# Moving lower-part subtractions between VectorE and GpSimd in the first 24 steps of a two-layer kernel

## The chip, the core and the metric

The kernel runs on one core of one Trainium2 chip. The metric is the device time of one execution in microseconds (us), given as the median of three runs. The engines are named as in the profile: PE is the matrix engine (TensorE) and PEld its weight loads, DVE is VectorE, ACT is ScalarE, POOL is GpSimd, and SP is SyncE, which only issues DMAs here. DMAs move data between the chip's memory and the on-chip memory SBUF. PE writes to PSUM, which has eight banks here: four for the first product of a step ("ps") and four for the second ("acc").

## The reference

The inputs are eight batches of eight heads with 576 positions of width 64, and two feed-forward layers with weights of 512 x 2048 and 2048 x 512 in float64 (they reach the kernel as pairs of 32-bit words).

```
q_s = exp(q - max(q, width));      q_s = q_s / sum(q_s, width)
k_s = exp(k - max(k, positions));  k_s = k_s / sum(k_s, positions)
x   = q_s @ (k_s^T @ v)                      # per head; 4608 tokens x 512
h   = x @ w_in;   g = where(h > 0, h, exp(min(h, 0)) - 1);   x = g @ w_out      # layer 1 (elu)
h   = x @ w2_in;  g = (a0 + a1 h + a2 h^2 + a3 h^3) / (1 + |b0||h| + |b1| h^2 + 1e-6)
out = g @ w2_out                                                                # layer 2 (rational)
```

## The kernel before, in words

**Blocks and steps.** The 4608 tokens are cut into nine blocks of 512 (index j), the 2048 hidden values into 16 slices of 128 (index f). A step is one layer, one block and one slice. Its "in" part makes h of 128 hidden values by 512 tokens in one ps bank (12 matmuls, L781 to L783), and its "out" part adds the slice's share to four acc banks (12 matmuls, L823). There are 144 steps in each layer. The list `tiles` sets their order; steps are numbered from 0 in that order, and I5 and O5 below are the in and out parts of step 5. Steps 0 to 3 are block 0 with slices 0 to 3, steps 4 to 11 are block 1 with slices 0 to 7, steps 12 to 23 finish block 0, and steps 24 to 31 finish block 1.

**Two parts of each number.** A float32 matrix is split into an upper part of fewer bits and a lower part, the difference. Each product is three matmuls: upper by upper, upper by lower, lower by upper. ACT makes the upper part (`copy_hi`, L299), and `sub_lo` (L302) subtracts it on the engine that it is given. So L302 stands for the lower part of an elu tile ("gs<-m,gs"), of an input tile ("xs<-ps,xs") or of weights ("w_in<-x,w_in" and "w_out<-x,w_out").

**An elu step.** When h is there, ACT makes relu(-h) in a tile m (L887) and its exponential (L890), DVE makes the elu from m and h and so frees the ps bank (L893), ACT makes the upper part in a tile gs (L299), and then comes the lower part from m and gs (L302), which frees m. Out matmuls read gs and free it. There are two m tiles, two gs tiles and four ps banks: the relu of a step waits for the lower part of the step two earlier, and an in part waits for the elu four earlier.

**Weights of layer 1.** They are loaded as 64-bit words in pairs of slices: one tile of 1 MB for w_in and one for w_out, so 16 tiles in all. A conversion is five operations: a guard of the high half words on DVE ("floor", L323), a scaling on ACT (L331), a shift on DVE (L327), a join on DVE (L335), the upper part on ACT (L299, 128 x 1024), and then the lower part (L302, 128 x 1024). Pair 0 is wanted at I0, pair 1 at I2, pairs 2 and 3 at I8 and I10, and the others at I16, I18, I20 and I22; the w_out tiles are wanted at the out parts of the same steps.

**Attention.** It is made beside the steps. For each pair of heads k goes through a maximum (L667), an exponential (L670), transposes (L679) and the product with v (L518); q goes through a maximum (L537), a subtraction (L560, POOL), an exponential (L564), a sum (L567), its reciprocal (L571, L572), a multiplication (L575, POOL) and transposes (L581). L637 then makes a block's x of two pairs of heads at a time, and ACT and DVE (L302, "xs<-ps,xs") split it.

**What sets the order.** The instructions are not written out in order. `op` registers an operation with the engines it may use, an estimated cost, what it waits for, the buffers that it takes and frees, and a rank. `Plan.run` then lists them: at each turn it starts the operation that can begin first by its own clock, and settles ties by due times that `set_due` works out backward from the order of the PE work. `EITHER` lets the planner choose POOL (1.4) or DVE (0.8). Each engine executes its list in order, so a waiting instruction holds up all behind it on that engine. L276 are matmuls of an identity that the planner puts in where it sees PE wait in the first 100 us.

Of the kernel before, what the change touches and what calls it, by code (L numbers as in the profile page):

```python
# [34 lines left out]
class Plan:  # L35
# [17 lines left out]
    def op(self, engines, fn, after=(), rank=0.0, take=(), free=(), extra=0.0, follow=(), dma=0.0):  # L53
        o = dict(lead=self.lead, rush=0.0, main=False, due=None, follow=[a for a in follow if a is not None], issued=None, engines=engines, fn=fn, after=[a for a in after if a is not None], rank=rank, take=take,
                 free=free, extra=extra, dma=dma, held={}, end=None, next=[], n=len(self.ops))
        waits = o["after"] + o["follow"]
        o["left"] = len(waits)
        for a in waits:
            a["next"].append(o)
        self.ops.append(o)  # L60
        return o
# [120 lines left out]
def linear_attention_elu_rational(  # L182
# [65 lines left out]
    op = plan.op  # L248
# [7 lines left out]
    def DVE(c=0.75):  # L256
        return (("DVE", c),)

    def ACT(c=0.62):
        return (("ACT", c),)  # L260

    def POOL(c=1.4):
        return (("POOL", c),)

    EITHER = (("POOL", 1.4), ("DVE", 0.8))
# [5 lines left out]
    def f32_tile(tag, bufs, pool=None):  # L271
        return (pool or main).tile([P, TB], F32, tag=tag, name=tag, bufs=bufs)
# [25 lines left out]
    def copy_hi(hi, src):  # L298
        nc.scalar.activation(out=hi, in_=src, func=AF.Copy)  # L299

    def sub_lo(e, lo, src, hi):
        engine[e].tensor_tensor(out=lo, in0=src, in1=hi.bitcast(F32), op=ALU.subtract)  # L302
# [4 lines left out]
    def new_slots(f, which):  # L307
        pair = main.tile([P, 2, 2, DM], F32R, tag=f"w{f // 2}_{which}", name=("w_in", "w_out")[which], bufs=1)
        for i in range(2):
            slot[f + i, which] = pair[:, i]  # L310
        return pair

    def whole(n):
        return 0.2 + n * 0.0006, 0.2 + n * 0.00116

    def plan_f32(st_op, st_of, new_x, n, rank, x_kinds, joined=None):

        b = {}
        fast, slow = whole(n)

        def floor(e):
            top = st_of().rearrange("p n t -> p (n t)").bitcast(I16).rearrange("p (n u) -> p n u", u=4)[:, :, 3]
            nc.vector.tensor_scalar(out=top, in0=top, scalar1=FLOOR, scalar2=None, op0=ALU.max)  # L323

        def low(e):
            t = st_of()[:, :, 0]
            nc.vector.tensor_scalar(out=t, in0=t, scalar1=29, scalar2=None, op0=ALU.logical_shift_right)  # L327

        def scale(e):
            b["x"] = new_x()  # L330
            nc.scalar.activation(out=b["x"], in_=st_of()[:, :, 1].bitcast(F32), func=AF.Prelu, scale=2.0**-112, alpha=-2.0**32)  # L331

        def join(e):
            xi = b["x"].bitcast(I32)
            nc.vector.scalar_tensor_tensor(out=joined().bitcast(I32) if joined else xi, in0=xi, scalar=3, in1=st_of()[:, :, 0], op0=ALU.logical_shift_left,  # L335
                                           op1=ALU.bitwise_or)

        o1 = op(DVE(slow), floor, [st_op], rank)
        o2 = b["own"] = op(ACT(0.25 + n * 0.00095), scale, [o1], rank, take=x_kinds)
        o3 = op(DVE(fast), low, [st_op], rank)  # L340
        return op(DVE(slow), join, [o2, o3], rank), b

    def plan_w1(f, which, rank, load_rank, after):

        w = (moe_w_in, moe_w_out)[which]
        kind = f"w{f // 2}_{which}"
        b = {}

        def load(e):
            b["st"] = main.tile([P, 2 * DM, 2], I32, tag=kind, name="bits", bufs=1)  # L350
            nc.sync.dma_start(out=b["st"].rearrange("p n t -> p (n t)"), in_=w[f // 2].bitcast(I32))

        def new_x():
            (name, _), = x["own"]["held"].items()
            return at.tile([P, 2 * DM], F32, tag=name, name="x", bufs=1)

        def pairs(ap):
            return ap.rearrange("p (i n) -> p i n", i=2)

        def hi(e):  # L360
            b["hl"] = new_slots(f, which)
            copy_hi(b["hl"][:, :, 0], pairs(x["x"]))

        def lo(e):
            sub_lo(e, b["hl"][:, :, 1], pairs(x["x"]), b["hl"][:, :, 0])

        b["op"] = op(SP, load, after, load_rank, take=[kind], dma=2.6)
        o, x = plan_f32(b["op"], lambda: b["st"], new_x, 2 * DM, rank, [("x", "st")])
        own = op(ACT(1.05), hi, [o], rank)
        o = op(DVE(1.4), lo, [own], rank, free=[(("x", "st"), x["own"])])  # L370
        at_ops.append(o)
        for i in range(2):
            slot_ready[0, f + i, which], slot_owner[0, f + i, which] = o, b["op"]
        return o
# [391 lines left out]
    def step_of(L, j, f):  # L766
        return place[L, j, f]

    def plan_in(t, b):
        L, j, f = t  # L770
        s = step_of(*t)

        def mm(kks):
            def fn(e):
                if 0 in kks:
                    b["h"] = bank()
                w = slot[f, 0].rearrange("p s (k c) -> p s k c", c=P)
                for kk in kks:
                    x = x_tile[L, j, kk]
                    o = turned(b["h"])  # L780
                    nc.tensor.matmul(o, w[:, 0, kk, :], two(x[:, 0]), start=(kk == 0), stop=False)  # L781
                    nc.tensor.matmul(o, w[:, 0, kk, :], two(x[:, 1]), start=False, stop=False)  # L782
                    nc.tensor.matmul(o, w[:, 1, kk, :], two(x[:, 0]), start=False, stop=(kk == KD - 1))  # L783
            return fn

        parts = [(i,) for i in range(KD)] if f in (0, KF - 1) else [tuple(range(KD))]
        o = None
        for n, kks in enumerate(parts):
            free = []
            if f == KF - 1:  # L790
                free += [(x_owner[L, j, kk][0], x_owner[L, j, kk][1]) for kk in kks]
            if j == NB - 1 and n == len(parts) - 1 and f % 2:
                free.append((f"w{f // 2}_0", slot_owner[L, f, 0]))
            o = op(PE(0.65 * len(kks)), mm(kks),
                   [last.get("mm_in"), slot_ready[L, f, 0]] + [x_ready[L, j, kk] for kk in kks],
                   s, take=["bank"] if n == 0 else [], free=free,
                   follow=[x_owner[L, j, kk][1] for kk in range(KD)] if n == 0 and f == 0 else [])
            o["main"] = True
            if n == 0:
                b["h_op"] = o  # L800
            last["mm_in"] = o
        in_ops[t] = o
        return o
# [77 lines left out]
    def plan_elu(t):  # L881
        b = {}
        s = step_of(*t)

        def relu(e):
            b["m"] = f32_tile("m", 2)
            nc.scalar.activation(out=b["m"], in_=b["h"], func=AF.Relu, scale=-1.0)  # L887

        def exp(e):
            nc.scalar.activation(out=b["m"], in_=b["m"], func=AF.Exp, scale=-1.0)  # L890

        def elu(e):
            nc.vector.scalar_tensor_tensor(out=b["m"], in0=b["m"], scalar=-1.0, in1=b["h"], op0=ALU.add, op1=ALU.max)  # L893

        def hi(e):
            b["g"] = main.tile([P, 2, TB], F32R, tag="gs", name="gs", bufs=2)
            copy_hi(b["g"][:, 0], b["m"])

        def lo(e):
            sub_lo(e, b["g"][:, 1], b["m"], b["g"][:, 0])  # L900

        o = plan_in(t, b)
        o1 = op(ACT(), relu, [o], s + 0.5, take=["m"])
        o = op(ACT(), exp, [o1], s + 0.6)
        o = op(DVE(), elu, [o], s + 0.7, free=[("bank", b["h_op"])])
        o2 = op(ACT(), hi, [o], s + 1.0, take=["gs"])
        b["g_op"] = op(EITHER, lo, [o2], s + 1.1, free=[("m", o1)])
        b["g_free"] = ("gs", o2)
        plan_out(t, b)

# [90 lines left out]
    for n in range(2 * KF):  # L1001
        f, which = divmod(n, 2)
        s = KF + 3 * n
# [9 lines left out]
    for f in range(KF):  # L1013
        for which in range(2):
            b = {}
# [6 lines left out]
            own = slot_owner.get((1, f - 1, which))  # L1022
# [12 lines left out]
            own = op(ACT(), hi, [l, own if f % 2 else None], r, take=[] if f % 2 else [kind])  # L1035
# [33 lines left out]
    with tc.manual_schedule():  # L1069
# [25 lines left out]
        o = op(SP, load_ab, [in_ops[0, 1, 0]], 0.0)  # L1095
        op(ACT(0.2), minus_a, [o, in_ops[0, 2, 0]], 0.0)
        o = op(ACT(0.2), abs_b1, [o, in_ops[0, 2, 0]], 0.0)
        o = op(DVE(0.1), seed_b1, [o], 0.0)
        for _ in range(3):
            o = op(DVE(0.5), heron, [o], 0.0)  # L1100
# [69 lines left out]
```

## Time and profile before

| what | us |
|---|---|
| three runs | 1595.84, 5881.48, 1594.9 |
| median | 1595.84 |
| profiled execution, its own time | 1596.48 |
| its span, first to last instruction | 1594.7 |
| PE busy | 1572.8 (99% of the span) |
| DVE busy | 1039.8 (65%) |
| ACT busy | 1041.5 (65%) |
| POOL busy | 763.6 (48%) |

PE is busy nearly throughout, and the others half to two thirds of the span. These shares are means over stages: in the first 130 us DVE is nearly as full as PE. An idle time in square brackets at a row's end is that of the engine before the instruction, with what ended it. Durations of matmuls overlap, since they are pipelined; one starts about every 0.216 us when nothing holds PE up.

### The profile page before, as it was taken

How to read it: one execution, taken by the hardware profiler on the slowest of the kernel's cores; microseconds unless marked ns; L12 is line 12 of the kernel's file. 1: busy time of each engine (PE TensorE's matmuls, PEld its weight loads, DVE VectorE, ACT ScalarE, POOL GpSimd, SP SyncE). 2: the span in 40 equal slices, each digit the busy share in tenths (PEclk: the TensorE clock that was granted, in tenths of full speed). 3: DMA queues.
4: the chain of work that ended last, by engine and by line, in shares of the span. 5: the costliest groups of instructions: out<-in, count | busy, mean ns of one | idle time of the engine just before them, and what ended most of it. 6: DMA issues, size and time to landing. Idle time of an engine off the chain costs nothing.

```text
span 1594.7 us, 22842 instructions
## 1 busy us (share of the span) xinstructions
PE 1572.8 (99%) x8370; PEld 1355.0 (85%) x8370; DVE 1039.8 (65%) x1624; ACT 1041.5 (65%) x1837; POOL 763.6 (48%) x552
## 2 busy tenths in 40 slices
PE   8999999999999999999999999999999999999998
PEld 7787888888888888888887888888888888888886
DVE  7887666564655556431227768687778687777776
ACT  6767655454655455444558767777777777777676
POOL 3333323232332222232657566656666656666554
PEclk9999999999999999999999999999999999999999
DMA  9513443232332322101422010101010000100000
GB/s 348 221 67 102 144 142 110 90 110 97 102 111 88 102 96 90 53 14 34 139 93 80 1 54 1 54 0 54 0 54 1 28 27 20 34 7 21 1 27 27
DMA packets 48784, 113.31 MB, mean 71 GB/s; under 512 B 5664, under 2 KB 5664, under 8 KB 46624
## 3 DMA queue, kind: packets, MB, share of 16 engines
q1 hardware_dynamic: 48672, 111.85, 20.3%
q8 instruction: 66, 1.08, 0.3%
q14 instruction: 46, 0.38, 0.1%
HBM read 82.47 MB, written 29.36 MB: 70 GB/s over the span
## 4 chain that ended last, share of the span: by engine, by line
PE 87%; issue 3%; ACT 3%; DVE 3%; POOL 2%; DMA 0%; POOLq 0%; SPq 0%; DVEq 0%; ACTq 0%
PE acc L823 43%; PE ps L781 14%; PE ps L782 14%; PE ps L783 14%; POOL gs L302 2%; PE ps L637 1%; PE ps L510 1%; ACT p L926 1%; ACT s L922 1%; ACT m L932 0%; DMA e<-in_q_dram 0%; ACT m L935 0%; DVE s L938 0%; DVE m L941 0%; ACT g L299 0%
## 5 line engine op out<-in xcount | busy, mean ns | idle before, releaser
L781 PE MATMUL ps<-xs,w_in 128*128 128x512 f32 x1152 | 439.6, 382 | 6.6 <-DVE m L893 3.6
L782 PE MATMUL ps<-xs,w_in 128*128 128x512 f32 x1152 | 438.5, 381 | 0.0
L783 PE MATMUL ps<-xs,w_in 128*128 128x512 f32 x1152 | 438.4, 381 | 0.0
L823 PE MATMUL acc<-gs,w_out 128*128 128x512 f32 x1728 | 403.9, 381 | 1.3 <-POOL gs L302 0.8
L823 PEld LDWEIGHTS acc<-gs,w_out 128*128 128x128 f32 x1728 | 324.0, 189 | 52.9 <-ACT gs L299 2.8
L302 POOL TENSOR_TENSOR gs<-m,gs 128x512 fp32r<-128x512 f32 x119 | 163.4, 1373 | 360.5 <-ACT gs L299 336.6
L781 PEld LDWEIGHTS ps<-xs,w_in 128*128 128x128 f32 x1152 | 218.7, 190 | 42.0 <-issue 6.5
L783 PEld LDWEIGHTS ps<-xs,w_in 128*128 128x128 f32 x1152 | 218.7, 190 | 31.3
L782 PEld LDWEIGHTS ps<-xs,w_in 128*128 128x128 f32 x1152 | 218.7, 190 | 31.3 <-DVE xs L302 0.3
L893 DVE SCALAR_TENSOR_TENSOR m<-m,ps 128x512 f32<-128x512 f32 x144 | 98.4, 684 | 207.2 <-ACT m L890 198.5
L302 POOL TENSOR_TENSOR gs<-p,gs 128x512 fp32r<-128x512 f32 x72 | 115.9, 1609 | 236.1 <-issue 197.5
L929 POOL TENSOR_TENSOR s<-s,m 128x512 f32<-128x512 f32 x144 | 218.5, 1517 | 16.9 <-ACT m L918 16.9
L823 PE MATMUL acc<-w_out,gs 128*128 128x512 f32 x864 | 202.4, 381 | 2.7 <-ACT gs L299 1.6
L823 PE MATMUL acc<-w_out,g 128*128 128x512 f32 x864 | 199.8, 379 | 0.5 <-POOL g L302 0.5
L887 ACT ACTIVATE m<-ps 128x512 f32<-128x512 f32 x144 | 85.8, 596 | 167.2 <-PE ps L783 126.9
L938 DVE SCALAR_TENSOR_TENSOR s<-s,m 128x512 f32<-128x512 f32 x144 | 142.6, 990 | 71.6 <-ACT m L935 71.6
L823 PEld LDWEIGHTS acc<-w_out,gs 128*128 128x128 f32 x864 | 162.9, 189 | 29.4 <-POOL gs L302 4.6
L823 PEld LDWEIGHTS acc<-w_out,g 128*128 128x128 f32 x864 | 163.2, 189 | 24.0 <-POOL g L302 0.9
L926 ACT ACTIVATE p<-ps,a_sb 128x512 f32<-128x512 f32 x144 | 112.2, 779 | 81.4 <-POOL gs L302 74.0
L299 ACT ACTIVATE gs<-m 128x512 fp32r<-128x512 f32 x144 | 90.4, 628 | 92.4 <-PE acc L823 78.5
L947 DVE SCALAR_TENSOR_TENSOR p<-p,a_sb,ps 128x512 f32<-128x512 f32 x144 | 107.4, 746 | 57.1 <-ACT m L918 57.0
L951 DVE SCALAR_TENSOR_TENSOR p<-p,a_sb,m 128x512 f32<-128x512 f32 x144 | 136.6, 949 | 2.1
(122 smaller groups left out, 1904.7 us busy)
## 6 DMA issues: line engine op xcount, KB each, us to landing
x<-e SPq DMA_DIRECT2D x36, 256.0 KB, 2.1
e<-x SPq DMA_DIRECT2D x36, 256.0 KB, 3.0
out_dram<-e SPq DMA_DIRECT2D x36, 256.0 KB, 2.0
bits<-in_moe_w_in_dram SPq DMA_DIRECT2D x8, 1024.0 KB, 10.4
bits<-in_moe_w_out_dram SPq DMA_DIRECT2D x8, 1024.0 KB, 12.3
st<-in_moe_w_in_dram SPq DMA_DIRECT2D x16, 512.0 KB, 4.4
w<-st SPq DMA_DIRECT2D x32, 256.0 KB, 2.0
st<-in_moe_w_out_dram SPq DMA_DIRECT2D x16, 512.0 KB, 4.7
```

Source lines behind the costliest of these rows:

```text
L299: nc.scalar.activation(out=hi, in_=src, func=AF.Copy)
L302: engine[e].tensor_tensor(out=lo, in0=src, in1=hi.bitcast(F32), op=ALU.subtract)
L781: nc.tensor.matmul(o, w[:, 0, kk, :], two(x[:, 0]), start=(kk == 0), stop=False)
L782: nc.tensor.matmul(o, w[:, 0, kk, :], two(x[:, 1]), start=False, stop=False)
L783: nc.tensor.matmul(o, w[:, 1, kk, :], two(x[:, 0]), start=False, stop=(kk == KD - 1))
L823: nc.tensor.matmul(turned(o), lhsT, two(rhs), start=(f == f0 and n == 0), stop=(f == f1 and n == 2))
L893: nc.vector.scalar_tensor_tensor(out=b["m"], in0=b["m"], scalar=-1.0, in1=b["h"], op0=ALU.add, op1=ALU.max)
L926: nc.scalar.activation(out=b["p"], in_=b["h"], func=AF.Identity, scale=a_sb[:, 3:4], bias=a_sb[:, 2:3])
L929: engine[e].tensor_tensor(out=b["s"], in0=b["s"], in1=b["a"], op=ALU.add)
L938: nc.vector.scalar_tensor_tensor(out=b["s"], in0=b["s"], scalar=1.0 + 1e-6, in1=b["a"], op0=ALU.add, op1=ALU.mult)
L947: nc.vector.scalar_tensor_tensor(out=b["p"], in0=b["p"], scalar=a_sb[:, 1:2], in1=b["h"], op0=ALU.add, op1=ALU.mult)
L951: nc.vector.scalar_tensor_tensor(out=b["p"], in0=b["p"], scalar=a_sb[:, 0:1], in1=b["a"], op0=ALU.add, op1=ALU.mult)
```

## The change

The planner's estimate for a guard, a shift or a join over n values on DVE falls by 0.1 us each (`whole`). The lower parts of all 16 weight tiles of layer 1 go from DVE (estimate 1.4) to POOL (estimate 2.5). The lower parts of elu tiles of steps 0 to 23, for which the planner could choose, are set to DVE (estimate 0.7); before the change it had put all 24 on POOL. Numbers that are computed stay the same.

```diff
     def whole(n):
-        return 0.2 + n * 0.0006, 0.2 + n * 0.00116
+        return 0.1 + n * 0.0006, 0.1 + n * 0.00116
...
         own = op(ACT(1.05), hi, [o], rank)
-        o = op(DVE(1.4), lo, [own], rank, free=[(("x", "st"), x["own"])])
+        o = op(POOL(2.5), lo, [own], rank, free=[(("x", "st"), x["own"])])
...
         o2 = op(ACT(), hi, [o], s + 1.0, take=["gs"])
-        b["g_op"] = op(EITHER, lo, [o2], s + 1.1, free=[("m", o1)])
+        b["g_op"] = op(DVE(0.7) if s < 24 else EITHER, lo, [o2], s + 1.1, free=[("m", o1)])
```

The planner makes other lists from this. On PE the parts I4 to I18 and O4 to O13 stand in the same order in both; after O13 the change puts I19 one part earlier. From about step 95 of 288 on, the lists of all engines are the same again, and so is the whole of layer 2.

POOL before, from the subtraction for the third q tile of block 1 on (L560 and L575 are the attention's, "gs" are elu tiles):

```order
L560 TENSOR_TENSOR qt<-qt,mx 128x512
L302 TENSOR_TENSOR gs<-m,gs 128x512
L575 TENSOR_TENSOR qt<-qt,mx 128x512
L560 TENSOR_TENSOR qt<-qt,mx 128x512
L302 TENSOR_TENSOR gs<-m,gs 128x512
```

and POOL in the change, from the first weight tile on:

```order
L302 TENSOR_TENSOR w_in<-x,w_in 128x2x512
L575 TENSOR_TENSOR qt<-qt,mx 128x512
L302 TENSOR_TENSOR w_out<-x,w_out 128x2x512
L560 TENSOR_TENSOR qt<-qt,mx 128x512
L302 TENSOR_TENSOR w_in<-x,w_in 128x2x512
L575 TENSOR_TENSOR qt<-qt,mx 128x512
L560 TENSOR_TENSOR qt<-qt,mx 128x512 x2
L575 TENSOR_TENSOR qt<-qt,mx 128x512
L302 TENSOR_TENSOR w_out<-x,w_out 128x2x512
```

Where an elu tile of 512 columns stood between two attention operations, a weight tile of 1024 columns stands now; behind this stretch POOL's list has one more L575 and then the other twelve weight tiles, ahead of the attention of block 2.

DVE before, from the elu (L893) of step 12 to that of step 14:

```order
L893 SCALAR_TENSOR_TENSOR m<-m,ps 128x512
L335 SCALAR_TENSOR_TENSOR x<-x,bits 128x1024 x2
L323 TENSOR_SCALAR bits<-bits 128x1024
L893 SCALAR_TENSOR_TENSOR m<-m,ps 128x512
L302 TENSOR_TENSOR w_in<-x,w_in 128x2x512
L302 TENSOR_TENSOR w_out<-x,w_out 128x2x512
L327 TENSOR_SCALAR bits<-bits 128x1024
L323 TENSOR_SCALAR bits<-bits 128x1024
L893 SCALAR_TENSOR_TENSOR m<-m,ps 128x512
```

and DVE in the change, between the same three elus:

```order
L893 SCALAR_TENSOR_TENSOR m<-m,ps 128x512
L335 SCALAR_TENSOR_TENSOR x<-x,bits 128x1024
L302 TENSOR_TENSOR gs<-m,gs 128x512
L327 TENSOR_SCALAR bits<-bits 128x1024
L335 SCALAR_TENSOR_TENSOR x<-x,bits 128x1024
L893 SCALAR_TENSOR_TENSOR m<-m,ps 128x512
L323 TENSOR_SCALAR bits<-bits 128x1024
L302 TENSOR_TENSOR gs<-m,gs 128x512
L327 TENSOR_SCALAR bits<-bits 128x1024
L893 SCALAR_TENSOR_TENSOR m<-m,ps 128x512
```

Two weight tiles have left the place between the elus of steps 13 and 14, and an elu tile's lower part stands in each of the two gaps.

## Rows read from the trace of the kernel before

**Rows 1.** Waits of PE: who waited for whom, us in total, times, longest.

```profile
PE ps L781 <- DVE m L893: 3.6, 2, 2.2
PE ps L781 <- DVE p L947: 3.0, 2, 2.8
```

**Rows 2.** Busy time by stretch: length, then each engine's us (instructions), clock, DMA.

```profile
20.00:65.80 45.80, 42.74 (x351) 34.37 (x349) 44.16 (x68) 34.71 (x58) 19.43 (x13) 1.00 0.66 252
118.80:131.30 12.50, 8.90 (x31) 6.62 (x30) 10.73 (x11) 9.67 (x12) 1.81 (x2) 0.86 0.33 110
```

**Rows 3.** Timeline of PE: start, duration, what; I4, I17 and I18 begin here.

```profile
65.83 0.48 PE L781 MATMUL ps<-xs,w_in 128*128 128x512 f32 x1
...
121.21 0.48 PE L781 MATMUL ps<-xs,w_in 128*128 128x512 f32 x1 [1.38 <-DVE m L893]
...
126.93 0.49 PE L781 MATMUL ps<-xs,w_in 128*128 128x512 f32 x1 [2.21 <-DVE m L893]
```

**Rows 4.** Timeline of DVE, early: first weight guard, lower parts of block 1's input.

```profile
13.60 0.69 DVE L537 TENSOR_REDUCE mx<-e 128x8 f32<-128x512 f32 x1 [1.24 <-DMA e<-in_q_dram]
...
17.10 1.28 DVE L323 TENSOR_SCALAR bits<-bits 128x1024 int16<-128x1024 int16 x1
...
62.63 1.32 DVE L302 TENSOR_TENSOR xs<-ps,xs 128x512 fp32r<-128x512 f32 x2
```

**Rows 5.** DVE groups by line in 16 to 62.6 us: busy us, mean ns, idle.

```profile
L302 DVE TENSOR_TENSOR w_out<-x,w_out 128x1024 fp32r<-128x1024 f32 x2 | 3.1, 1530 | 0.0
...
L302 DVE TENSOR_TENSOR w_in<-x,w_in 128x1024 fp32r<-128x1024 f32 x2 | 2.5, 1234 | 0.0
```

**Rows 6.** Busy time from step 4's elu to step 13's, columns as in Rows 2.

```profile
70.90:120.40 49.50, 48.16 (x221) 41.23 (x219) 41.58 (x36) 32.56 (x41) 18.28 (x8) 1.00 0.31 128
```

**Rows 7.** DVE groups by line in that stretch, columns as in Rows 5.

```profile
L335 DVE SCALAR_TENSOR_TENSOR x<-x,bits 128x1024 int32<-128x1024 int32 x8 | 13.3, 1672 | 1.1 <-ACT x L331 0.7
L323 DVE TENSOR_SCALAR bits<-bits 128x1024 int16<-128x1024 int16 x7 | 10.7, 1522 | 0.0
L327 DVE TENSOR_SCALAR bits<-bits 128x1024 int32<-128x1024 int32 x6 | 6.7, 1134 | 0.0
...
L302 DVE TENSOR_TENSOR w_in<-x,w_in 128x1024 fp32r<-128x1024 f32 x3 | 4.7, 1576 | 0.2 <-ACT w_in L299 0.2
L302 DVE TENSOR_TENSOR w_out<-x,w_out 128x1024 fp32r<-128x1024 f32 x3 | 3.7, 1225 | 0.2 <-ACT w_out L299 0.2
```

**Rows 8.** POOL group by line in that stretch, columns as in Rows 5.

```profile
L302 POOL TENSOR_TENSOR gs<-m,gs 128x512 fp32r<-128x512 f32 x8 | 18.3, 2285 | 39.1 <-ACT gs L299 39.1
```

**Rows 9.** Timeline of DVE: a guard, a pair of joins, the queue before step 14's elu.

```profile
104.96 2.42 DVE L323 TENSOR_SCALAR bits<-bits 128x1024 int16<-128x1024 int16 x1
...
113.84 3.02 DVE L335 SCALAR_TENSOR_TENSOR x<-x,bits 128x1024 int32<-128x1024 int32 x2
116.72 1.37 DVE L323 TENSOR_SCALAR bits<-bits 128x1024 int16<-128x1024 int16 x1
120.47 0.69 DVE L893 SCALAR_TENSOR_TENSOR m<-m,ps 128x512 f32<-128x512 f32 x1 [2.37 <-ACT m L890]
121.07 1.22 DVE L302 TENSOR_TENSOR w_in<-x,w_in 128x1024 fp32r<-128x1024 f32 x1
122.21 2.31 DVE L302 TENSOR_TENSOR w_out<-x,w_out 128x1024 fp32r<-128x1024 f32 x1
...
126.16 0.71 DVE L893 SCALAR_TENSOR_TENSOR m<-m,ps 128x512 f32<-128x512 f32 x1
```

**Rows 10.** Timeline of POOL: two lower parts of elu tiles, steps 9 and 11.

```profile
103.90 2.29 POOL L302 TENSOR_TENSOR gs<-m,gs 128x512 fp32r<-128x512 f32 x1 [5.82 <-ACT gs L299]
...
114.04 5.03 POOL L302 TENSOR_TENSOR gs<-m,gs 128x512 fp32r<-128x512 f32 x1 [3.53 <-ACT gs L299]
```

**Rows 11.** Tile gs up to 180 us: duration ns min, median, max; first, last start.

```profile
L302 POOL TENSOR_TENSOR gs<-m,gs x24: 1276/1380/5032, 36.5 to 174.7; 128x512 fp32r<-128x512 f32 x24
```

**Rows 12.** Timeline of DVE: a lower part of an elu tile on DVE, later.

```profile
206.77 0.68 DVE L302 TENSOR_TENSOR gs<-m,gs 128x512 fp32r<-128x512 f32 x1
```

## The prediction

> **What bounds the kernel now.** I read the page's shares first: PE is busy for 1572.8 us of a span of 1594.7, so the end moves only where PE starts its work earlier or loses less. Next came PE's waits [rows 1]. The reader is to see two entries: 3.6 us for two in parts that waited for an elu (L893, layer 1), and 3.0 us for two that waited for layer 2's DVE work (L947). The second lies where the lists are unchanged, so I let it stand. The first belongs to the change, and PE's timeline places it [rows 3]: I17 waited 1.38 us and I18 2.21 us. The table by stretch shows what this cost (the later stretch of [rows 2]): in 12.5 us PE did 31 matmuls at a granted clock of 0.86. Undisturbed, 221 matmuls took 48.16 us [rows 6], 0.218 us each, so 31 are worth 6.8 us, and 5.7 us were lost. The waits make 3.6 of that. A mean clock of 0.86 over 12.5 us is 3.5 us at the lower level (1.2 of 2.4 GHz), which costs about 1.8 more.
>
> The other loss is at the start. From 20 to 65.8 us DVE was busy for 44.16 of 45.8 us (the earlier stretch of [rows 2]), and PE, though it shows 42.74, filled much of it with identity matmuls and small attention products. I4, the first step on block 1, began at 65.83 [rows 3], just behind the lower parts of block 1's input on DVE, whose first pair stood at 62.63 [rows 4]. From I4 to I17 PE had work without a break worth naming: 48.16 of 49.5 us [rows 6]. So two things count: when I4 starts, and what is lost at I17 and I18.
>
> **Term 1, up to I4.** I count what stands on DVE ahead of block 1's first input pair. Before: six guards, five shifts, five joins, four weight lower parts. After: five, five, four, none, and four elu lower parts. Removed are a guard (1.52) and a join (1.67, [rows 7]), and weight parts of 3.1 + 2.5 = 5.6 us [rows 5]; added are four elu parts at 0.68 [rows 12], 2.7 us. That is -6.1 us. The first guard (1.28) also moves ahead of the maximum at 13.60, into DVE's idle time of 1.24 us before it [rows 4], if its weights have landed by then; another -1.3: -7.4 us if DVE's amount alone decides.
>
> Against it: four weight parts now run on POOL. POOL shows no tile of 1024 columns. An undisturbed elu part takes it 1.28 us [rows 11]; twice that, 2.56, is the upper bound. On DVE the step from 512 to 1024 columns is 0.68 to 1.22 us [rows 9, 12], a factor of 1.79, which gives 2.30 as the lower one. I take 2.43, the middle. POOL then holds what the two engines share for 4 x 2.43 = 9.7 us in place of 4 x 1.28 = 5.1, up to 4.6 us of DVE's time, and the first two weight tiles come 1.2 us later each behind their join. That leaves -7.4 + 4.6 + 2.4 = -0.4, say 0, as the other end. I take the middle, **-3.7 us**.
>
> **Term 2, from step 4's elu to step 13's.** Between those two elus the change's list has two joins and two shifts more than the old one, eight elu lower parts, and no weight lower part (six before). That is 2 x 1.67 + 2 x 1.13 + 8 x 0.68 - (4.7 + 3.7) = +2.6 us [rows 7, 12]. Now the shared port. That the two engines exclude each other can be read: the guard at 104.96 took 2.42 us, against 1.28 for the first one, because POOL's elu part ran until 106.19 [rows 4, 9, 10]; and POOL's part for step 11 took 5.03 us, since DVE ran two joins and a guard beside it [rows 9, 10]. In this stretch POOL held the port for 8 x 1.28 = 10.2 us; nine weight tiles need 9 x 2.43 = 21.9, which is 11.7 us more. What can cover it: nine elus of 0.69 us [rows 9], 6.2 us, which read one tile from PSUM and one from SBUF. DVE's idle 49.5 - 41.58 = 7.9 us [rows 6] covers the rest if DVE fills it. DVE then needs 41.58 + 2.6 + 5.5 to 11.7 = 49.7 to 55.9 us where it took 49.5: +0.2 to +6.4. Nothing says how often POOL meets an elu, so I take the middle, **+3.3 us**. A gain is not in the bounds because DVE has as much of its own to do and POOL more.
>
> A rule of the Trainium skill speaks against the change here (SBUF — State Buffer, section "Who interferes with whom"): whichever engine issues first keeps the shared pair for its whole instruction, and the other blocks fully. By it every weight part on POOL would block DVE for its full length, and this term would be its upper end, +6.4 us. The trace agrees at 104.96, and differs at 114.04, where POOL got in only after three DVE instructions, not after the first.
>
> **Term 3, from step 13's elu to step 14's.** Before, two weight parts, a shift and a guard stood there: 121.07 to 126.16, 5.1 us [rows 9]. After: a guard, an elu part, a shift, 1.52 + 0.68 + 1.13 = 3.3 us. That is **-1.8 us**, with ends of -2.5 (the guard and shift undisturbed) and +0.6 (one whole weight part of POOL in the way).
>
> **What costs nothing.** The relu of step 13 no longer waits for POOL's 5.03 us; that wait is part of DVE's idle 2.37 us before the elu at 120.47 [rows 9], already spent as cover in term 2. A weight tile ready later on POOL is covered by lead: those of pairs 4 to 7 are wanted from I16 on, and their joins come several steps earlier; gone is that cover if POOL falls more than about two tiles (5 us) behind. POOL's attention work now queues behind a weight tile in place of an elu tile; that is in term 1's ends. The DMAs stay 16 weight loads; four attention loads swap places with neighbours, at a time when DVE is the later one. Estimates of the planner cost nothing themselves.
>
> **Sum.** -3.7 + 3.3 - 1.8 = -2.2 us at I18. PE has no wait from there to layer 2 in either list that the profile would let me expect, and one half-clock period follows the wait as before. The profiled execution took 1596.48 us, 0.64 above the median of 1595.84; so 1594.3 by its own time, and **1593.6 us** as a median.
>
> **Rivals.**
>
> *The stall disappears (1586.4).* The elu's lower part leaves POOL's queue, where it took 2.29 us on average [rows 8] against 0.68 on DVE, and elus 13 and 14 come in time. Then term 1 stays and the 5.7 us are saved: -9.4. For it: I17's wait ran from POOL's 5.03 us over relu and exponential to the elu. Against it: DVE's amount of work up to step 13's elu does not fall.
>
> *The port decides (1602.8).* Every weight tile on POOL blocks DVE for its whole length: term 1 gives 0, term 2 +6.4, term 3 +0.6, so +7.0, at the waits of I17 and I18. It decides from the point where about 10.8 of the 11.7 us extra are not covered, if term 1 holds, and from 6.9 if term 1 gives nothing. For it: at least 16 x 2.43 = 39 us of POOL in a stretch where DVE is nearly full. Against it: POOL waits too, as at 114.04, and that costs DVE nothing.
>
> *The start does not move (1597.3).* If I4 hangs on attention's chain of small steps over four engines, and not on DVE's amount, term 1 is 0 and the sum +1.5. For it: PE shows 42.74 us busy of the 45.8 before I4. Against it: DVE stood idle for 1.6 of them, and PE's share holds identity matmuls [rows 2].
>
> **How the numbers follow.** My forecast's own range is 1590 to 1596, chance 0.40. The start that does not move has 0.15, the vanished stall 0.20, the port 0.25. The range of 1586 to 1603 takes in the first two, most of the spread of 2 us about the third, and about half of the port's case, whose blocked waits may bring a second half-clock period: about 0.8 in all. A difference of 2% is 32 us, about what a measurement of this kernel can tell from no change; no case comes near it, and the 0.03 outside is for a wait that repeats over many steps (0.02) or a gain that I do not see (0.01).
>
> **What would show it.** Term 1: I4 starts near 62.1 us. Term 2: step 13's elu starts 49 to 56 us after step 4's; weight parts on POOL take 2.3 to 2.6 us undisturbed and some over 4. Term 3: about 3.5 us between the elus of steps 13 and 14. The loss at I17 and I18: PE's first wait longer than 1.38 us, the second shorter than 2.21. I am wrong if PE waits for a weight tile (L302 on POOL), if waits turn up behind step 24, or if layer 2's 3.0 us changes.

## The result: slower, at a ratio of 1.0056, and the profile after

The changed kernel took 1602.16 us (median of 5 runs, 1600.33 to 1604.01), the kernel before 1594.9 us in the same comparison; the ratio is 1.0056, 95% interval 1.0045 to 1.0067, so some 7 to 11 us slower. One of before's five executions took 5881.48 us and is left out of the ratio. The result is on the other side of the forecast of 1593.6, inside the range, and 0.6 us from the rival in which the port decides (1602.8). The interval is 0.2% wide, so this measurement tells differences far smaller than the 2% that the prediction took for its limit.

The profiled execution took 1600.33 us, with a span of 1598.5: only 3.8 above the span of before, 1594.7. The two spans must not be subtracted as they stand. Both executions have layer 2's wait of 2.8 us, but in that of before a stretch at the lower clock follows it and in that of after none does. The row of before (length, then each engine's busy us and instructions in the order PE, PEld, DVE, ACT, POOL, then clock and DMA):

```profile
856.00:876.00 20.00, 17.17 (x67) 14.25 (x66) 16.67 (x19) 15.24 (x26) 15.85 (x11) 0.83 0.13 41
```

and three stretches of after, the last of them around the same place:

```profile
72.20:125.60 53.40, 47.33 (x214) 39.66 (x212) 49.58 (x42) 36.36 (x44) 26.06 (x8) 1.00 0.20 86
129.00:144.80 15.80, 11.72 (x47) 9.73 (x46) 9.27 (x11) 9.26 (x15) 4.70 (x2) 0.89 0.68 219
860.00:880.00 20.00, 17.15 (x80) 14.74 (x79) 17.48 (x20) 14.06 (x24) 16.24 (x11) 1.00 0.19 53
```

A clock of 0.83 over 20 us is 6.8 us at the lower level (1.2 of 2.4 GHz) and costs about 3.4. So the change is read ahead of this place. The matmul with which PE resumes after layer 2's wait begins 6.9 us later in after:

```profile
861.92 0.77 PE L781 MATMUL ps<-xs,w_in 128*128 128x512 f32 x1 [2.83 <-DVE p L947]
868.77 0.45 PE L781 MATMUL ps<-xs,w_in 128*128 128x512 f32 x1 [2.85 <-DVE p L947]
```

The first two rows of after answer to [rows 6] and to the later stretch of [rows 2]: from step 4's elu to step 13's it is now 53.4 us in place of 49.5, PE has gaps of 6 us in it where it had 1.3, and DVE is busy for 49.58 us in place of 41.58.

PE's waits of after (who waited for whom, us in total, times, longest), to be set against [rows 1]:

```profile
PE ps L781 <- DVE m L893: 9.3, 4, 4.1
PE ps L781 <- DVE p L947: 3.0, 2, 2.8
```

and PE's timeline (start, duration, what, the wait ahead of it), against [rows 3]:

```profile
64.25 0.48 PE L781 MATMUL ps<-xs,w_in 128*128 128x512 f32 x1
67.05 0.48 PE L782 MATMUL ps<-xs,w_in 128*128 128x512 f32 x1 [1.02 <-DVE xs L302]
107.82 0.45 PE L781 MATMUL ps<-xs,w_in 128*128 128x512 f32 x1 [1.77 <-DVE m L893]
121.62 0.45 PE L781 MATMUL ps<-xs,w_in 128*128 128x512 f32 x1 [2.12 <-DVE m L893]
126.48 0.45 PE L781 MATMUL ps<-xs,w_in 128*128 128x512 f32 x1 [1.38 <-DVE m L893]
134.03 0.77 PE L781 MATMUL ps<-xs,w_in 128*128 128x512 f32 x1 [4.08 <-DVE m L893]
```

These are I4's first pair, its second pair, and then I14, I16, I17 and I18. I4 begins 1.6 us earlier than before, waits inside, and four waits for an elu stand where two stood: 9.3 us in place of 3.6. I18 begins at 134.03 in place of 126.93, 7.1 us later. Nothing behind it adds to this: from I18 to the end after's execution needs 1464.5 us and before's 1467.8, of which some 3.4 go to its slower clock in layer 2.

In between PE is level in both. I7, and the out part ahead of I14, begin at the same time to within 0.1 us (the first of each pair of lines is before's):

```profile
75.39 0.38 PE L781 MATMUL ps<-xs,w_in 128*128 128x512 f32 x1
75.45 0.38 PE L781 MATMUL ps<-xs,w_in 128*128 128x512 f32 x1
...
103.23 2.75 PE L823 MATMUL acc<-gs,w_out 128*128 128x512 f32 x12
103.30 2.75 PE L823 MATMUL acc<-gs,w_out 128*128 128x512 f32 x12
```

So what I4 gained was gone by I7, and the whole loss arises from I14 to I18: 5.3 us stand at I17 (126.48 in place of 121.21), and 1.8 more come at I18.

DVE's timeline of after, with the places that answer to [rows 4, 9]:

```profile
59.27 1.29 DVE L302 TENSOR_TENSOR xs<-ps,xs 128x512 fp32r<-128x512 f32 x2 [0.23 <-ACT xs L299]
60.74 1.32 DVE L323 TENSOR_SCALAR bits<-bits 128x1024 int16<-128x1024 int16 x1
...
64.94 1.46 DVE L335 SCALAR_TENSOR_TENSOR x<-x,bits 128x1024 int32<-128x1024 int32 x1 [0.55 <-ACT x L331]
66.28 1.31 DVE L302 TENSOR_TENSOR xs<-ps,xs 128x512 fp32r<-128x512 f32 x2
...
69.03 3.38 DVE L335 SCALAR_TENSOR_TENSOR x<-x,bits 128x1024 int32<-128x1024 int32 x1 [0.19 <-ACT x L331]
72.24 0.77 DVE L893 SCALAR_TENSOR_TENSOR m<-m,ps 128x512 f32<-128x512 f32 x1
...
87.13 1.62 DVE L335 SCALAR_TENSOR_TENSOR x<-x,bits 128x1024 int32<-128x1024 int32 x1
88.59 0.76 DVE L302 TENSOR_TENSOR gs<-m,gs 128x512 fp32r<-128x512 f32 x1
89.18 1.43 DVE L323 TENSOR_SCALAR bits<-bits 128x1024 int16<-128x1024 int16 x1
...
125.65 0.68 DVE L893 SCALAR_TENSOR_TENSOR m<-m,ps 128x512 f32<-128x512 f32 x1
126.25 3.03 DVE L323 TENSOR_SCALAR bits<-bits 128x1024 int16<-128x1024 int16 x1
129.07 2.81 DVE L302 TENSOR_TENSOR gs<-m,gs 128x512 fp32r<-128x512 f32 x1
...
133.20 0.69 DVE L893 SCALAR_TENSOR_TENSOR m<-m,ps 128x512 f32<-128x512 f32 x1 [0.72 <-ACT m L890]
```

and POOL's at the same places, against [rows 10]:

```profile
67.56 3.36 POOL L302 TENSOR_TENSOR w_in<-x,w_in 128x1024 fp32r<-128x1024 f32 x1 [11.81 <-DMA b_sb<-in_moe_b_dram]
...
87.62 5.06 POOL L302 TENSOR_TENSOR w_out<-x,w_out 128x1024 fp32r<-128x1024 f32 x1 [3.74 <-ACT w_out L299]
92.64 2.37 POOL L302 TENSOR_TENSOR w_in<-x,w_in 128x1024 fp32r<-128x1024 f32 x1
...
125.72 2.38 POOL L302 TENSOR_TENSOR w_in<-x,w_in 128x1024 fp32r<-128x1024 f32 x1 [6.66 <-ACT w_in L299]
128.04 3.29 POOL L302 TENSOR_TENSOR w_out<-x,w_out 128x1024 fp32r<-128x1024 f32 x1
```

The two are read side by side by their ends. POOL's tile of 125.72 ends at 128.10 and the guard that DVE began at 126.25 takes until 129.28, 3.03 us for an instruction of 1.28. POOL's next tile ends at 131.33, and DVE's lower part of 0.68 us takes 2.81, until 131.88. Step 14's relu waits for that part (it frees m), the elu for the relu, and I18 for the elu. ACT's timeline has the relu:

```profile
131.91 0.60 ACT L887 ACTIVATE m<-ps 128x512 f32<-128x512 f32 x1 [4.57 <-DVE gs L302]
```

### The profile page after: what moved, and what is told of

It reads as the page before. It is cut to its first block, busy times and chain, and to the rows that moved or that the text cites. A ratio compares the mean times of both kernels' runs of the same rounds, so it can differ in the third digit from the quotient of the medians.

```text
span 1598.5 us, 22806 instructions
## 1 busy us (share of the span) xinstructions
PE 1568.2 (98%) x8348; PEld 1349.9 (84%) x8348; DVE 1053.8 (66%) x1646; ACT 1037.8 (65%) x1823; POOL 769.9 (48%) x544
## 4 chain that ended last, share of the span: by engine, by line
PE 86%; DVE 4%; ACT 4%; issue 3%; POOL 2%; DMA 1%; POOLq 0%; SPq 0%; DVEq 0%; ACTq 0%
PE acc L823 43%; PE ps L781 14%; PE ps L782 14%; PE ps L783 14%; PE ps L637 1%; PE ps L510 1%; DVE x L335 1%; ACT p L926 1%; POOL gs L302 1%; DVE gs L302 1%; ACT s L922 1%; POOL w_out L302 1%; ACT x L331 0%; DVE bits L327 0%; ACT m L932 0%
## 5 line engine op out<-in xcount | busy, mean ns | idle before, releaser
L302 POOL TENSOR_TENSOR gs<-m,gs 128x512 fp32r<-128x512 f32 x95 | 122.7, 1291 | 293.2 <-ACT gs L299 279.2
L893 DVE SCALAR_TENSOR_TENSOR m<-m,ps 128x512 f32<-128x512 f32 x144 | 98.6, 684 | 197.4 <-ACT m L890 190.5
```

## Experiments

Three edits make up the change: the planner's estimates of a whole conversion (0.1 in place of 0.2), the weights' lower parts on POOL, and the elu tiles' lower parts of steps 0 to 23 on DVE. The first runs are the change with some of them undone; each diff is against the changed kernel unless it says otherwise. The runs were compared with the kernel before in three groups, in which its median was 1593.51, 1592.91 and 1592.19 us (1594.9 with the change), so differences of 1 or 2 us between runs of different groups are not read. Theory 1 is the port, theory 2 the amount of DVE's work, theory 3 the estimates and theory 4 weights that come late from POOL.

**The elu parts alone.**

```diff
-        return 0.1 + n * 0.0006, 0.1 + n * 0.00116
+        return 0.2 + n * 0.0006, 0.2 + n * 0.00116
-        o = op(POOL(2.5), lo, [own], rank, ...
+        o = op(DVE(1.4), lo, [own], rank, ...
```

> Of the change only the elu lower parts of steps 0 to 23 go to VectorE; weight lower parts and estimates stay as before. Theory 1 (port): the 16 weight tiles of 2.4 to 5 us on GpSimd are what blocks VectorE; without them GpSimd holds the shared port only for attention, so the waits of PE at I17 and I18 shrink from 9.3 us to under 4, and the time is 1588 to 1595. Theory 2 (amount of VectorE work): 24 elu parts add 16 us to a VectorE that is nearly full, and nothing leaves it, so this is the slowest part: 1602 to 1610, with elu waits of PE above 9 us.

Measured: 1589.62 us, ratio 0.9981 (0.9972 to 0.999). With more on DVE than before the kernel is faster, so the amount of DVE's work is not what slows the change down.

**The change without the weights.**

```diff
-        o = op(POOL(2.5), lo, [own], rank, ...
+        o = op(DVE(1.4), lo, [own], rank, ...
```

> The change without its move of the weight lower parts (they stay on VectorE): elu parts on VectorE and lower estimates. Theory 1 (port): 1588 to 1596, that is 6 us or more below the changed kernel; guards, shifts and joins take at most 1.6 us each from step 4 on. Theory 2 (amount): VectorE has 19 us more of its own work than in the changed kernel, 1604 or more. Theory 3 (lower estimates pack guards and joins ahead of elus and of block 1's input): as the changed kernel, 1600 to 1604.

Measured: 1586.61 us, 0.9957 (0.9943 to 0.9971). This is faster than both kernels and below every range that was expected, and the one line that is undone is worth 15.6 us. Its stretch from step 4's elu to step 13's, which answers to [rows 6], and its DVE groups there (line, what, count, busy us, mean ns, idle before and its releaser):

```profile
68.70:111.50 42.80, 42.80 (x200) 37.46 (x200) 37.68 (x39) 32.14 (x40) 0.00 (x0) 1.00 0.35 147
...
L335 DVE SCALAR_TENSOR_TENSOR x<-x,bits 128x1024 int32<-128x1024 int32 x6 | 9.2, 1533 | 1.4 <-ACT x L331 1.2
L323 DVE TENSOR_SCALAR bits<-bits 128x1024 int16<-128x1024 int16 x6 | 8.0, 1333 | 0.0
L302 DVE TENSOR_TENSOR gs<-m,gs 128x512 fp32r<-128x512 f32 x8 | 5.5, 687 | 2.2 <-ACT gs L299 2.2
L327 DVE TENSOR_SCALAR bits<-bits 128x1024 int32<-128x1024 int32 x4 | 4.0, 999 | 0.0
L302 DVE TENSOR_TENSOR w_in<-x,w_in 128x1024 fp32r<-128x1024 f32 x3 | 3.7, 1229 | 0.0
```

POOL does nothing here, PE has no gap, and DVE is at 37.68 of 42.8 us although the elus' and the weights' lower parts are both on it. The same groups in the changed kernel, 72.2 to 125.6:

```profile
L335 DVE SCALAR_TENSOR_TENSOR x<-x,bits 128x1024 int32<-128x1024 int32 x10 | 18.4, 1837 | 3.4 <-ACT x L331 3.3
L327 DVE TENSOR_SCALAR bits<-bits 128x1024 int32<-128x1024 int32 x8 | 13.8, 1722 | 0.0
L323 DVE TENSOR_SCALAR bits<-bits 128x1024 int16<-128x1024 int16 x7 | 11.0, 1568 | 0.0
L302 DVE TENSOR_TENSOR gs<-m,gs 128x512 fp32r<-128x512 f32 x8 | 7.8, 977 | 0.0
```

The same instructions take longer: a join 1837 ns in place of 1533, a shift 1722 in place of 999, a guard 1568 in place of 1333, an elu tile's lower part 977 in place of 687.

**Old estimates, and each of the other edits by itself.** Three runs complete the set.

```diff
-        return 0.1 + n * 0.0006, 0.1 + n * 0.00116
+        return 0.2 + n * 0.0006, 0.2 + n * 0.00116
```

> The change without its lower estimates: weight lower parts on GpSimd, elu parts on VectorE. Theory 1 (port): the same holds of the port, 1600 to 1605. Theory 3 (estimates): without them guards and joins are placed as far apart as before, 1593 to 1597.

Measured: 1601.49 us, 1.005 (1.0036 to 1.0064).

```diff
-        return 0.1 + n * 0.0006, 0.1 + n * 0.00116
+        return 0.2 + n * 0.0006, 0.2 + n * 0.00116
-        b["g_op"] = op(DVE(0.7) if s < 24 else EITHER, lo, ...
+        b["g_op"] = op(EITHER, lo, ...
```

> Of the change only the weight lower parts go to GpSimd; for elu parts the planner may choose either engine, and puts most of those of steps 0 to 23 on GpSimd too. Theory 1 (port): the most port time on GpSimd of all (16 x 2.4 us and the elu parts), and elu parts queue behind weight tiles: 1600 to 1612. Theory 4 (late weights): as the changed kernel, 1600 to 1603. If the move of the weights is right in itself: under 1594.

Measured: 1600.14 us, 1.0048 (1.0035 to 1.006).

```diff
-        o = op(POOL(2.5), lo, [own], rank, ...
+        o = op(DVE(1.4), lo, [own], rank, ...
-        b["g_op"] = op(DVE(0.7) if s < 24 else EITHER, lo, ...
+        b["g_op"] = op(EITHER, lo, ...
```

> Of the change only the lower estimates of guards, shifts and joins. Theory 1 (port): nothing moves between engines, GpSimd's elu part of step 11 may still be starved: 1590 to 1597. Theory 3 (estimates): 1598 or more.

Measured: 1593.74 us, 1.0009 (1.0 to 1.0018). The estimates alone are worth nothing, and at most 3.0 us beside the elu parts (1589.62 to 1586.61; 1.6 by the table below). The weights on POOL cost 7.2 us on the kernel before (1592.91 to 1600.14), 11.9 beside the elu parts (1589.62 to 1601.49) and 15.6 beside both; theory 3 falls. Beside the elu parts, where the kernel is faster without them, they take more away.

**The port by itself.** Weights back on DVE, as in the run without them, and in POOL's list at each place of a weight tile two subtractions of 512 columns whose result nobody reads. The other engines' lists are the same as in that run.

```diff
-        o = op(POOL(2.5), lo, [own], rank, ...
+        o = op(DVE(1.4), lo, [own], rank, ...
+        def hold(e):
+            scratch = at.tile([P, DM], mybir.dt.bfloat16, ...)
+            for i in range(2):
+                upper = b["hl"][:, i, 0].bitcast(F32)
+                nc.gpsimd.tensor_tensor(out=scratch, in0=upper, in1=upper, op=ALU.subtract)
+        at_ops.append(op(POOL(0.0), hold, [own], rank))
```

> As 'without weights' (1586.6 us), with the same lists on PE, VectorE, ScalarE and SyncE; on GpSimd alone two subtractions of 512 columns are added behind each weight tile's upper part, 32 in all, into a scratch tile that nobody reads. No weight, elu tile or buffer waits for them. Theory 1 (the port is what costs): VectorE is blocked as in the halved tiles (1604.8), so 1597 to 1606, with guards, shifts and joins of over 2 us again. Theory 4 (weights come later and their source buffer is freed later, so VectorE's joins wait for ScalarE): the added work hinders nobody, 1586 to 1589.

Measured: 1599.63 us, 1.0044 (1.003 to 1.0057). Work that nothing waits for costs 13.0 us, where the change's weights on POOL cost 15.6. PE's waits and, below them, the stretch and DVE's groups from step 4's elu to step 13's (72.5 to 121.4, so 48.9 us in place of 42.8; the lines stand 8 lower, and the elu is L901):

```profile
PE acc L831 <- DVE gs L302: 4.9, 3, 2.4
PE ps L789 <- DVE m L901: 4.0, 2, 2.9
PE ps L789 <- DVE p L955: 3.0, 2, 2.8
...
72.50:121.40 48.90, 48.64 (x225) 41.95 (x223) 45.75 (x40) 31.78 (x40) 21.19 (x14) 1.00 0.31 129
...
L323 DVE TENSOR_SCALAR bits<-bits 128x1024 int16<-128x1024 int16 x6 | 10.4, 1730 | 0.0
L335 DVE SCALAR_TENSOR_TENSOR x<-x,bits 128x1024 int32<-128x1024 int32 x6 | 10.3, 1712 | 1.4 <-ACT x L331 1.2
L302 DVE TENSOR_TENSOR gs<-m,gs 128x512 fp32r<-128x512 f32 x8 | 8.1, 1007 | 0.0
L901 DVE SCALAR_TENSOR_TENSOR m<-m,ps 128x512 f32<-128x512 f32 x10 | 6.8, 684 | 0.9 <-ACT m L898 0.8
L327 DVE TENSOR_SCALAR bits<-bits 128x1024 int32<-128x1024 int32 x4 | 4.7, 1180 | 0.0
```

The counts of guards, joins, elu parts and shifts are those of the run without weights (6, 6, 8, 4), and only the durations grew: 6 x 0.40 + 6 x 0.18 + 8 x 0.32 + 4 x 0.18 = 6.8 us. With the weights' lower parts, which grew too, DVE is busy for 8.1 us more (45.75 in place of 37.68) and idle for 2.0 less, which makes the 6.1 by which the stretch is longer.

POOL's attention work queues behind the added instructions as well, and this could slow a run without any port. The trace speaks against it. Block 1's first input pair stands on DVE 3.8 us later (64.95 in place of 61.14), but from 16 to 56 us DVE is idle for 1.1 us where it was for 1.7; what grew are durations, as of a weight's lower part (2.09 us at 25.01 in place of 1.25).

So POOL's mere running is enough for most of the price, and theory 1 is shown as the main cause. The 13.0 us are no exact share: an added pair takes 2.54 us undisturbed where a weight tile takes 2.37, and DVE still has the weights to do. Theory 4 has a part too, which the trace of the changed kernel shows. ACT's scaling of the next weight waits until POOL's slow tile of 87.62 has ended and freed its source, and DVE's join at 94.33 waits 2.62 us for that scaling. These are ACT's scaling, and DVE's waits for scalings from 60 to 135 us in the changed kernel and in the run without weights (us, times, longest):

```profile
92.72 1.58 ACT L331 ACTIVATE x<-bits 128x1024 f32<-128x1024 f32 x1 [1.73 <-POOL w_out L302]
...
DVE x L335 <- ACT x L331: 4.7, 5, 2.6
...
DVE x L335 <- ACT x L331: 1.9, 3, 0.8
```

What these waits cost by themselves no run shows.

**Half the weights.** Only the w_out tiles on POOL.

```diff
-        o = op(POOL(2.5), lo, [own], rank, ...
+        o = op(POOL(2.5) if which else DVE(1.4), lo, [own], rank, ...
```

> The changed kernel with only the w_out tiles on GpSimd, eight of 16; the w_in tiles stay on VectorE. Theory 1 (port): about half of the 15 us between 'without weights' (1586.6) and the change (1602.2): 1591 to 1598. Theory 4 (late weights): w_out is wanted two to three steps later than w_in and has the most lead, so hardly a loss: 1586 to 1590.

Measured: 1594.04 us, 1.0005 (0.9996 to 1.0013). Halfway between 1586.6 and 1602.2 is 1594.4: by the medians eight tiles cost half of what sixteen do. By the table below they cost a third (4.8 of 14.9 us), so that the price goes evenly by the number of tiles is not shown.

**Halved tiles.** Each weight tile's lower part on POOL as two instructions of 512 columns.

```diff
-            sub_lo(e, b["hl"][:, :, 1], pairs(x["x"]), b["hl"][:, :, 0])
+            for i in range(2):
+                sub_lo(e, b["hl"][:, i, 1], pairs(x["x"])[:, i], b["hl"][:, i, 0])
```

> The changed kernel with each weight lower part on GpSimd cut in two instructions of 512 columns, everything else in the same order. Theory 1 in its form 'one long hold at the wrong moment': VectorE gets in after 1.28 us, elu 13 to elu 14 falls from 7.5 to about 5 us, and the time falls by 3 to 5 us to 1597 to 1599. Theory 1 in its form 'sum of holds': the sum is the same or a little more, so 1600 to 1604.

Measured: 1604.76 us, 1.007 (1.0057 to 1.0083), a little above what either form of theory 1 expected. Shorter holds, twice as many, help nothing; that fits the sum of the time, and not the length of one hold.

**The hold in the plan.** The planner adds to an operation of DVE that uses the port the whole time that POOL still needs, in place of at most a quarter of the operation's own cost.

```diff
-            if e == "DVE" and t < UNTIL:
-                cost += SHARED * min(cost, max(0.0, self.free_at.get("POOL", 0.0) - t))
+            if e == "DVE" and t < UNTIL and o["fn"].__name__ in ("floor", "low", "join", "lo", "q_rec"):
+                cost += max(0.0, self.free_at.get("POOL", 0.0) - t)
```

> The changed kernel, planned with the whole time that GpSimd still holds the port added to a guard, shift, join, reciprocal or lower part on VectorE (before: at most a quarter of the operation's own cost). Theory 1 in its form 'sum of holds' (the port's time is lost wherever the tiles stand): 1598 to 1604. Theory 1 in its form 'placing' (the planner puts weight tiles between elus because it does not know the price): 1588 to 1596.

Measured: 1597.01 us, 1.0031 (1.002 to 1.0041). That is just between the two ranges expected. A list made with the hold in it gives 5 of the 15.6 us back, and some 10 stay. So part of the price lies in where the holds fall; that the rest is their sum is argued and not shown, for no run has another list.

The same rule of the planner, with this edit beside it:

```diff
-        o = op(POOL(2.5), lo, [own], rank, ...
+        o = op(DVE(1.4), lo, [own], rank, ...
```

> 'Without weights' (1586.6) with the same planning rule. GpSimd has attention work alone up to step 24, so theory 1 expects little: 1584 to 1589 in both forms; a gain of 3 us or more would say that attention's holds also delay block 1's input.

Measured: 1589.39 us, 0.9974 (0.9965 to 0.9984), 2.8 above the run without the rule. It is not a better rule in itself: what it gives back above comes from the weights on POOL.

**How far the elu parts should go.** Both without the weights on POOL, up to step 40 and up to step 15; the diffs are against the run without the weights.

```diff
-        b["g_op"] = op(DVE(0.7) if s < 24 else EITHER, lo, ...
+        b["g_op"] = op(DVE(0.7) if s < 40 else EITHER, lo, ...
```

> 'Without weights' with the elu lower parts of steps 0 to 39 on VectorE in place of 0 to 23. After step 24 PE has no waits, so theory 1 (the gain comes from the steps beside the conversions) expects 1585 to 1588. If elu parts on VectorE were good in themselves: under 1585.

Measured: 1586.91 us, 0.9963 (0.995 to 0.9976).

```diff
-        b["g_op"] = op(DVE(0.7) if s < 24 else EITHER, lo, ...
+        b["g_op"] = op(DVE(0.7) if s < 15 else EITHER, lo, ...
```

> 'Without weights' with elu lower parts of steps 0 to 14 alone on VectorE. Conversions run until about step 14 or beyond; if what helps is an undisturbed VectorE up to I18 (theory 1), 1585 to 1589; if the steps behind it count as well, 1589 to 1593.

Measured: 1589.68 us, 0.9981 (0.9971 to 0.999). Steps 24 to 39 are worth nothing, and steps 15 to 23 at most 3.1 us, of which the table below has 1.2.

Of all kernels the change without the weights is the fastest, together with its form up to step 40: the elu tiles' lower parts of the first 24 steps on DVE, and the new estimates. No run gives the weights' source tiles another buffer, which would test theory 4 by itself.

**The runs at one place of PE's list.** Executions of one kernel differ by some us in what the clock does behind layer 2's wait. From PE's first matmul after that wait to the end the profiled executions need 729.7 to 733.7 us: 729.7 in the changed kernel's, where the clock stays at 1.00 behind it, and 732.8 in before's (0.50 over the first 4 us, 0.74 over the next 4). So the start of this matmul is a second measure beside the median. It comes from one execution of each kernel, and how far it spreads was not measured.

| kernel | start, us | against before |
|---|---|---|
| before | 861.92 | 0 |
| the change | 868.77 | +6.9 |
| elu parts alone | 855.49 | -6.4 |
| without the weights | 853.85 | -8.1 |
| old estimates | 867.72 | +5.8 |
| weights alone | 866.85 | +4.9 |
| estimates alone | 860.21 | -1.7 |
| port by itself | 866.50 | +4.6 |
| half the weights | 858.69 | -3.2 |
| halved tiles | 871.72 | +9.8 |
| hold in the plan | 863.51 | +1.6 |
| the same, without the weights | 856.08 | -5.8 |
| elu parts to step 40 | 853.67 | -8.3 |
| elu parts to step 15 | 855.05 | -6.9 |

The weights on POOL cost 14.9 us by it, and the port by itself 12.7. The theories that fall do so by it too; the small steps (estimates, steps 15 to 23) shrink to what one execution can hardly tell.

## Why the prediction was wrong, point by point

The sum was -2.2 us at I18, and +7.1 came. Counted from elu to elu, as the prediction did, term 1 was 5.0 us off, term 3 3.7 and term 2 0.6. So two steps failed: in term 1 that the first input pair decides when block 1 gets going, and in term 3 that at most one weight part of POOL stands in the way.

**Term 3: its assumption of one hold.** The time between the elus of steps 13 and 14 was to fall from 5.69 us by 1.8, with +0.6 as the worst end ("one whole weight part of POOL in the way"). It rose to 7.55, by +1.9. There were two weight parts in the way, back to back (125.72 and 128.04), each held one DVE instruction, and the second held the one that the relu waits for. What I missed is that the old list had its two weight parts on DVE just here, that POOL had only 1.81 us of work in the 12.5 us around this place [rows 2], and that moving the weights put 5.7 us of POOL's time (2.38 + 3.29) just where DVE had been almost free of it.

**Term 1: right up to the first pair, lost by the second.** The first input pair stood on DVE at 59.27 in place of 62.63, -3.4 us for a forecast of -3.7. But I4 needs the second pair too. It came at 66.28 in place of 66.58, since two guards, two shifts and a join of the weights stand between the pairs in the new list; PE waited 1.02 us in I4. I had counted what stands ahead of the first pair only. PE, which began I4 1.6 us earlier, was level with before at I7 (75.45 and 75.39). Then step 4's elu came at 72.24 in place of 70.9, because the join of 69.03 took 3.38 us behind POOL's tile (67.56 to 70.92). So term 1 gave +1.3 from elu to elu in place of -3.7, and nothing on PE.

**Term 2: right in size, by two misses that cancel.** 72.24 to 125.65 is 53.4 us in place of 49.5: +3.9, for a forecast of +3.3 between +0.2 and +6.4. DVE's busy time rose by 8.0 us, the 2.6 of the list and 5.4 of holds, and its idle time fell only from 7.9 to 3.8. The holds were at the low end (5.5), and the cover that every bound took as full was used only by half. That the middle came so near is luck. On PE this stretch lost more, 5.3 us up to I17. The prediction had nine weight tiles in it; eight ran. A weight part on POOL took 2.37 us undisturbed (92.64; the estimate was 2.43).

The three sum to +1.3 + 3.9 + 1.9 = +7.1, the 7.1 us at I18.

Two slips in the prediction's figures change nothing: the second point from which the port would decide comes out at 7.1 us by its own sum, not 6.9, and its sign of term 3, about 3.5 us between the elus, does not agree with 5.69 - 1.8 = 3.9.

**The rivals.** That the port decides was right in mechanism, and in size as a sum (+7.1 for +7.0) by parts that make up for each other: term 2 came below its upper end, and the two others beyond theirs; that elus wait at I14 and I16 too was not in it. The vanished stall was wrong as a whole for this kernel, and right for its elu edit: with that edit and the estimates, the run without the weights took 1586.61 us where the rival gave 1586.4. Against before in its own group that is 6.9 us less, and 8.1 by the table, for a forecast of 9.4, so the nearness of the two times is partly luck. The reason that I gave against it, DVE's amount of work, was wrong, for there DVE has more instructions and still leaves PE without a gap. That the start does not move was wrong for I4, which began 1.6 us earlier, and, with another cause, right for what follows.

The Trainium skill (SBUF — State Buffer, section "Who interferes with whom") has it that the later of two engines at the shared pair waits for the other's whole instruction. The trace agrees for DVE, at 126.25 and 129.07, and it differs for POOL at 87.62, where a tile of 2.37 us took 5.06 beside three DVE instructions and went on when DVE stood idle. By the rule in full I would have taken the upper ends, +7.0; I took the middle because of the places where POOL waits, and those don't lower what DVE pays elsewhere.

**What cost nothing.** It held that PE waits for no weight tile on POOL, that layer 2's wait stays (3.0 us, 2.8 at most), and that nothing new stands behind step 24. The half-clock period behind I18 came as before: 0.89 over 129 to 144.8.

## What to carry to other kernels

Work that leaves a nearly full VectorE for GpSimd does not leave it if the two share a port: sixteen parts of 1.23 us on VectorE cost 15.6 us more as parts of 2.37 us on GpSimd, and 32 instructions of GpSimd that nobody waits for cost 13.0. Count a hold for every instruction of GpSimd that meets a VectorE queue, and look at which instructions it meets: two tiles back to back at a place where a short chain decides cost more than their average. Where a stage begins with several inputs, time the last of them, not the first.

## What was unexpected of the hardware

The two engines did not wait alike. In the changed kernel DVE waited through at most one POOL instruction each time, while POOL's tile at 87.62 needed 5.06 us. The elu, which reads one tile from PSUM, was hardly touched: 684 ns on average in the port's run, where a guard grew from 1333 to 1730. And one and the same wait of 2.8 us in layer 2 was followed by a stretch at the lower clock in before's execution (0.83 on average over 20 us) and by none in after's (1.00), which makes some 3 us at the end.
